# Taking 1/std out of the first MLP layer's input, and making the MLP matmuls narrower, in a one-core decode kernel

## The chip, the core and the metric

The kernel runs on one core of a Trainium2 chip. The metric is the device time of one execution in microseconds (us). Each execution is also reported with a "span", the time from the first to the last instruction of the program. Repeated executions of one kernel agree within some tenths of a microsecond out of 671 (the four of the kernel before within 0.18 us), so the noise is about 0.05%.

PE is the tensor engine, DVE the vector engine, ACT the scalar engine, POOL is GpSimd, SP the engine that issues most DMAs. SBUF is the memory that the kernel's transfers fill and its engines work from. Instructions wait for semaphores, which other instructions and transfers raise (in the trace a chunk of W2 does so in 16 steps). The granted clock is the share of its full speed that the tensor engine's clock was given, as the trace records it.

## The reference

A transformer block for 8 sequences, one new token each: a modulation from `c`, attention over a cache of 8192 keys and values, then an MLP. What matters here is the end:

```
x = x + ga * attention(...)                       # called x1 below
h = layernorm(x) * (1 + cb) + sb                  # layernorm: (x - mean) / sqrt(var + 1e-5)
hid = relu(h @ w1 + b1) ** 2                      # 512 -> 1792
x = x + gb * (hid @ w2 + b2)                      # 1792 -> 512
```

The two caches are 268 MB in bf16. `w1` and `w2` are 1.84 MB each.

## The kernel before

Keys and values stream through a ring of four SBUF slots, 4 MB per transfer, all issued by SP in one queue. The order of that queue at the end is: the last 4 MB of V in four pieces, then W1 in two, then W2 in four.

```python
d_w1 = [dma("sync", s_w1[i], ... W1v[:, a:z], w1_r[:, a:z] ...)
        for i, (a, z) in enumerate(((0, 3), (3, 4)))]
d_w2 = [dma("sync", s_w2[i], ...)          # rows f of W2, 128 each
        for i, (a, z, j) in enumerate(((0, 4, 4), (4, 8, 4), (8, 12, 4), (12, 14, 2)))]
```

After the last attention matmul and the output projection comes the tail. Activations are kept transposed (features on partitions, the batch of 8 in columns), and each weight tile of 128x128 is the stationary operand of one matmul. `wide` repeats the 8 columns four times, so that a matmul has 32 columns, of which 8 are used.

```python
t = vector(xcT = x1T - mean);  k_xc = t
t = vector(sqT = xcT * xcT)
t = vector(sqs = sum of sqT over k)
t = tensor(var_ps = ONESM.T @ sqs)                 # sum over partitions
k_xcb = vector(xcb = xcT * cb1)                    # cb1 = 1 + cb
t = scalar(std2 = sqrt(var_ps + eps))
t = vector(rstd2 = 1 / std2)
t = vector(h1T = xcb * rstd2)
k_hb = vector(hbT = h1T + mod(3))                  # mod(3) = sb
for ks in (range(KT - 1), range(KT - 1, KT)):      # KT = 4, FT = 14
    for f in range(FT):
        for k in ks:                               # waits for k_hb and W1's piece
            t = tensor(hT_w[f] += W1[k, f].T @ wide(hbT[k]))
        if k == KT - 1 and f % 7 == 6:             # one half of f is complete
            t = vector(rT = max(hT, 0));  k_sq.append(vector(hidT = rT * rT))
for f in range(FT):
    for k in range(KT):                            # waits for k_sq[f // 7] and d_w2[f // 4]
        t = tensor(yT_w[k] += W2[f, k].T @ wide(hidT[f]))
k_y2 = vector(y2T = yT * mod(5))                   # then two small transposes, copy, DMA out
```

(Shortened: every line is one instruction with its dependencies. The listing at the end of this section has the full text.)

Of the kernel before, what the change touches and what calls it, by code (L numbers as in the profile page):

```python
# [5 lines left out]
ACT = mybir.ActivationFunctionType  # L6
ALU = mybir.AluOpType
AX = mybir.AxisListType
FP32 = mybir.dt.float32
BF16 = mybir.dt.bfloat16  # L10
# [20 lines left out]
class Prog:  # L31
# [19 lines left out]
    def op(self, eng, fn, deps=(), chan=None):  # L51
        chan = chan or eng
        assert self.of[chan] == eng
        t = Tok(self.sems[chan], chan, self.at)
        t.used = chan in ("vecP", "scaP")
        self.ops[eng].append(Op(fn, deps, t, None, self.at))
        return t
# [95 lines left out]
def bass_adaLN_cond__gqa_block_cached__dense_activation_squared_relu__decode_kernel(  # L153
    nc, A_x, A_k_cache, A_v_cache, A_wq, A_wo, B_x, B_w1, B_b1, B_w2, B_b2, c, w_mod, out):
    B, _, D = A_x.shape
    _, HKV, SK, DH = A_k_cache.shape
# [4 lines left out]
    KT = D // 128  # L161
# [9 lines left out]
    with ExitStack() as es:  # L171
        E = es.enter_context
        sb = lambda name, shape, dt: E(nc.sbuf_tensor(name, shape, dt))
# [18 lines left out]
        IDENT = sb("IDENT", [128, 128], BF16)  # L192
# [6 lines left out]
        ONESM = sb("ONESM", [128, 128], FP32)  # L199
        ONESMB = sb("ONESMB", [128, 128], BF16)  # L200
        ONE8 = sb("ONE8", [1, B], BF16)
        PERM = sb("PERM", [128, 4, 32], BF16)
        oP = sb("oP", [128, 4, 6, B], BF16)
        epst = sb("epst", [128, 1], FP32)
# [8 lines left out]
        cb1 = sb("cb1", [128, KT, B], FP32)  # L213
        tmpT = sb("tmpT", [128, KT, B], FP32)
        haT = sb("haT", [128, KT, B], BF16)
        b1_row = sb("b1_row", [1, F], BF16)
# [3 lines left out]
        xcT = sb("xcT", [128, KT, B], FP32)  # L220
        sqT = sb("sqT", [128, KT, B], FP32)
        sqs = sb("sqs", [128, B], FP32)
        xcb = sb("xcb", [128, KT, B], FP32)
        std2 = sb("std2", [128, B], FP32)
        rstd2 = sb("rstd2", [128, B], FP32)
        h1T = sb("h1T", [128, KT, B], FP32)
        hbT = sb("hbT", [128, KT, B], BF16)
        hidT = sb("hidT", [128, FT, B], BF16)
        out_sb = sb("out_sb", [128, 256], BF16)

# [7 lines left out]
        rT = KF[:, 1024:1024 + 2 * FT * B].bitcast(FP32).rearrange("p (f b) -> p f b", f=FT)  # L238
# [7 lines left out]
        bank = lambda i: PS[:, i, :]  # L246
# [4 lines left out]
        op, dma = Pg.op, Pg.dma  # L251
# [34 lines left out]
        t = pool(lambda e: e.memset(ONE8[:], 1.0))  # L286
# [6 lines left out]
        t = select(IDENT[:], [[-1, 128]], 0, 1, 1.0, NE, t)  # L293
        t = select(IDF8[:], [[-1, 8]], 0, 1, 1.0, NE, t)
        k_id = t
        k_q0 = pool(lambda e: e.memset(QTm[:], 0.0))
        t = pool(lambda e: e.memset(Pm[:], 0.0), [t])
        k_pm = t
        for d in (-96, -64, -32, 0, 32, 64, 96):
            t = select(R4[:], [[-1, 128]], -d, 1, 1.0, NE, t)  # L300
        t = select(Qmask[:], [[-32, 4]], 0, 1, 0.0, GE, t)
        t = select(Qmask[:], [[32, 4]], 31, -1, 0.0, GE, t)
        for d in (0, 32, 64, 96):
            t = select(R4m[:], [[-1, 32]], -d, 1, 1.0, NE, t)

        for i in range(4):
            for cg in range(4):
                for half in range(2):
                    t = select(SEL[:, i, 4 * half:4 * half + 4], [[-1, 4]], -(32 * cg + 8 * i + 4 * half), 1,
                               1.0, NE, t)  # L310

        t = select(PERM[:], [[-1, 4], [-4, 32]], 0, 1, 1.0, NE, t)
# [31 lines left out]
        for k in range(KT):  # L344
            t = op("tensor", lambda e, k=k: e.matmul(csT_ps[:, k, :], cs_k[:, k, :], IDENT[0:B, 0:B],
                                                    is_transpose=True), [k_cs, k_id])
# [3 lines left out]
        for k in range(KT):  # L350
            t = op("tensor", lambda e, k=k: e.matmul(xT_ps[:, k, :], x_sb[:, k * 128:(k + 1) * 128],
                                                    IDENT[0:B, 0:B], is_transpose=True), [d_x])
        k_xT = op("vector", lambda e: e.tensor_copy(xT[:], xT_ps), [t])
        t = op("vector", lambda e: e.bn_stats(stats[:], x_sb), [d_x])
        t = op("vector", lambda e: e.bn_aggr(mv[:], stats[:]), [t])
        t = op("vector", lambda e: e.tensor_scalar(std_[:], mv[:, 1:2], EPS, None, ALU.add), [t])
        t = op("scalar", lambda e: e.activation(std_[:], std_[:], ACT.Sqrt), [t])
        t = op("vector", lambda e: e.reciprocal(rstd[:], std_[:]), [t])
        t = op("vector", lambda e: e.tensor_scalar(hn, x_sb, mv[:, 0:1], rstd[:, 0:1], ALU.subtract, ALU.mult), [t])
# [14 lines left out]
        for j in range(24):  # L374
            for k in range(KT):
                t = op("tensor", lambda e, j=j, k=k: e.matmul(
                    modT_ps[:, j, :], wm_cols(k, j), csT[:, k, :],
                    start=(k == 0), stop=(k == KT - 1)), [k_csT, d_wm])
        released[2] = t
        k_modT = op("vector", lambda e: e.tensor_copy(modT[:], modT_ps), [t])  # L380
        mod = lambda j: modT[:, KT * j:KT * (j + 1), :]
        t = op("vector", lambda e: e.tensor_scalar(ca1[:], mod(1), 1.0, None, ALU.add), [k_modT])
        t = op("vector", lambda e: e.tensor_tensor(tmpT[:], hnT_ps, ca1[:], ALU.mult), [t, k_hnT])
# [8 lines left out]
        for g in range(HKV):  # L392
            r0 = 16 * (g % 2) + 4 * (g // 2)
            k_QTm = op("vector", lambda e, g=g, r0=r0: e.tensor_copy(
                QTm[:, :, g, r0:r0 + REP], QT_ps[:, REP * g:REP * (g + 1), :].rearrange("p h b -> p b h")),
                [t, k_q0])
        k_cb1 = op("vector", lambda e: e.tensor_scalar(cb1[:], mod(4), 1.0, None, ALU.add))

        stg_free = [None, None, None, k_QTm]
# [14 lines left out]
        kt_read = [None, None]  # L414
        qn = 0
        norm_last = None

        def pe_fill(n, at=7):
            for _ in range(n):
                op("tensor", lambda e: e.matmul(bank(at)[:, 0:128], IDENT[:, :], IDENT[:, :]))  # L420

        def pe_stream(n, at):
            rhs = IDENT[:, :].unsqueeze(1).to_broadcast([128, 4, 128])
# [32 lines left out]
        def fcol(ap, f):  # L456
            a, j = (4 * (f // 4), 4) if f < F2 else (F2, 2)
            return ap[:, 128 * a:128 * (a + j)].rearrange("o (p j) -> o j p", j=j)[:, f - a, :]
# [1 line left out]
        wide = lambda ap: ap.unsqueeze(1).to_broadcast([128, 4, B])  # L460
        attn_w = bank(4)[:, 0:32 * KT].rearrange("p (k a b) -> p k a b", k=KT, a=4)
        attn_ps = attn_w[:, :, 0, :]
        hT_w = [bank(i)[:, 0:32 * 7].rearrange("p (f a b) -> p f a b", f=7, a=4) for i in range(2)]
        hT_ps = [h[:, :, 0, :] for h in hT_w]
        yT_w = bank(2)[:, 0:32 * KT].rearrange("p (k a b) -> p k a b", k=KT, a=4)
        yT_ps = yT_w[:, :, 0, :]

        def early(q0, q1, deps):
            nq = q1 - q0
# [18 lines left out]
        for b in range(B):  # L488
# [4 lines left out]
            for p in range(NP):  # L493
                n = 2 * NP * b + p
# [65 lines left out]
            for p in range(NP):  # L560
# [4 lines left out]
                if not lastu:  # L565
# [21 lines left out]
                    if lastb and p == 1:  # L587
                        k_oP = early(0, 2, [norm_last, k_all] + stg_free + hold)
                        for f in range(FT):
                            op("tensor", lambda e, f=f: e.matmul(  # L590
                                hT_ps[f // 7][:, f % 7, :], fcol(b1_row[:], f), ONE8[:, :],
                                start=(f % 7 == 0), stop=False, skip_group_check=True), [d_b2, s_bank_free[f // 7]])
                        project(0, 2, k_oP)
                    if lastb and p == 2:
# [67 lines left out]
        bc = lambda ap: ap.unsqueeze(1).to_broadcast([128, KT, B])  # L662
        t = op("vector", lambda e: e.tensor_tensor(xcT[:], x1T[:], bc(mean_ps), ALU.subtract), [t])
        k_xc = t
        t = op("vector", lambda e: e.tensor_tensor(sqT[:], xcT[:], xcT[:], ALU.mult), [t])
        t = op("vector", lambda e: e.tensor_reduce(sqs[:], sqT[:].rearrange("p k b -> p b k"), AX.X, ALU.add), [t])
        var_ps = bank(5)[:, 0:B]
        t = op("tensor", lambda e: e.matmul(var_ps, ONESM[:, :], sqs[:]), [t])  # L668
        k_xcb = op("vector", lambda e: e.tensor_tensor(xcb[:], xcT[:], cb1[:], ALU.mult), [k_xc])
        t = op("scalar", lambda e: e.activation(std2[:], var_ps, ACT.Sqrt, bias=epst[:, 0:1]), [t])  # L670
        t = op("vector", lambda e: e.reciprocal(rstd2[:], std2[:]), [t])
        t = op("vector", lambda e: e.tensor_tensor(h1T[:], xcb[:], bc(rstd2[:]), ALU.mult), [t, k_xcb])
        k_hb = op("vector", lambda e: e.tensor_tensor(hbT[:], h1T[:], mod(3), ALU.add), [t])
        k_sq = []
        wcol = lambda k, f: fcol(W1v[:, k, :], f)
        for ks in (range(KT - 1), range(KT - 1, KT)):
            for f in range(FT):
                for k in ks:
                    t = op("tensor", lambda e, f=f, k=k: e.matmul(  # L679
                        hT_w[f // 7][:, f % 7, :, :], wcol(k, f), wide(hbT[:, k, :]), start=False, stop=(k == KT - 1),  # L680
                        skip_group_check=True), [k_hb, d_w1[k // (KT - 1)]])
                if k == KT - 1 and f % 7 == 6:
                    hh = f // 7
                    fs = slice(7 * hh, 7 * (hh + 1))
                    t = op("vector", lambda e, hh=hh, fs=fs: e.tensor_scalar(
                        rT[:, fs, :], hT_ps[hh], 0.0, None, ALU.max), [t])
                    k_sq.append(op("vector", lambda e, fs=fs: e.tensor_tensor(
                        hidT[:, fs, :], rT[:, fs, :], rT[:, fs, :], ALU.mult), [t]))
        for f in range(FT):
            for k in range(KT):  # L690
                t = op("tensor", lambda e, f=f, k=k: e.matmul(  # L691
                    yT_w[:, k, :, :], W2v[:, f, k * 128:(k + 1) * 128], wide(hidT[:, f, :]),
                    start=False, stop=(f == FT - 1), skip_group_check=True), [k_sq[f // 7], d_w2[f // 4]])
        k_y2 = op("vector", lambda e: e.tensor_tensor(y2T, yT_ps, mod(5), ALU.mult), [t])
        outf = out.rearrange("b s d -> (b s) d")
# [45 lines left out]
```

## Time and profile before

| | before |
|---|---|
| time, median of 4 runs | 671.10 us (670.93 to 671.11) |
| span of the profiled run | 668.9 us |
| mean DMA rate | 424 GB/s |
| tail, from the start of x - mean to the start of the final multiply by gb | 659.3 to 666.0 us |

From the page of the kernel before: the busy share of the DMA engines and what they moved, in 40 equal slices of the span.

```profile
DMA  9999999999999999999999999999999999999996
GB/s 371 434 401 432 429 427 435 435 425 429 437 435 425 435 427 435 435 427 429 433 439 425 434 431 434 433 425 431 437 435 425 426 439 437 423 433 431 437 409 259
```

The DMA engines are at work through all of the run, at 424 GB/s on average, and they fall off in the last slice alone (16.7 us long). The kernel is bound by moving its 284 MB.

The timeline of the kernel before, in the tail. Columns: start in us, duration in us, engine, line, operation, output<-input, shapes, count, and in brackets how long the engine had been idle and what ended that.

```profile
660.04 0.60 PE L668 MATMUL PS<-sqs,ONESM 128*128 128x8 f32 x2 [0.53 <-DVE sqs L666]
660.67 0.27 ACT L670 ACTIVATE std<-PS,epst 128x8 f32<-128x8 f32 x1 [23.79 <-PE PS L668]
660.97 0.20 DVE L671 RECIPROCAL rstd<-std 128x8 f32<-128x8 f32 x1 [0.89 <-ACT std L670]
661.43 0.19 DVE L673 TENSOR_TENSOR hbT<-h1T,modT 128x32 bf16<-128x32 f32 x1
661.68 2.00 PE L679 MATMUL PS<-hbT,ring 128*128 128x32 bf16 x56 [1.05 <-DVE hbT L673]
664.01 1.91 PE L691 MATMUL PS<-hidT,ring 128*128 128x32 bf16 x56 [0.34 <-DVE hidT L687]
665.96 0.19 DVE L694 TENSOR_TENSOR KTb<-PS,modT 128x32 bf16<-128x32 f32 x1 [1.62 <-PE PS L691]
```

Read alone, this says that engines set the pace: layer 1 (L679) waits for hbT, which waits for 1/std; layer 2 (L691) waits for hidT. It is a nearly complete serial chain, and it looks as if whatever is cut out of it comes off the end. The chain of waits of the same kernel has one odd place, where layer 2 is in two pieces:

```profile
664.01 1.50 PE PS L691 x48
665.51 0.01 issue
665.52 0.41 PE PS L691 x8
```

48 matmuls and then 8. The first 48 use chunks 1 to 3 of W2 (f = 0 to 11), the last 8 use chunk 4. The starts of the matmuls in the trace show 26.7 ns between most, and 195 ns between the 48th and the 49th. (There is a slight wait for chunk 3 as well: 41 and 46 ns before the 33rd and the 34th.) The trace's DMA completion events say why. Each of these transfers has 16 of them, as many as the profile counts DMA engines, and they come apart: those of chunk 4 from 661.63 to 665.47 us, 3.8 us in all. The landing is the last of the 16:

```
last landing, us      V's last piece   W1 k=0..2   W1 k=3   W2 chunk 1   chunk 2   chunk 3   chunk 4
before                656.67           660.05      661.17   662.43       663.65    664.86    665.47
```

The 49th matmul starts at 665.52, 0.05 us behind chunk 4's landing.

### The profile page before, as it was taken

The page shows a single profiled execution, that of the slowest core. Times are in us where ns is not written, and L with a number is a line of the kernel's source. Part 1 is how long each engine was busy: PE and PEld are TensorE (multiplying, and loading weights), DVE is VectorE, ACT ScalarE, POOL GpSimd, SP SyncE. Part 2 cuts the span into 40 slices and gives each one's busy share as a digit, 9 for nine tenths or more (in the row PEclk, how much of TensorE's full clock was granted, in tenths as well). Part 3 has the DMA queues.
Part 4 walks back from the last instruction along what each step waited for, and adds up shares of the span by engine and source line. Part 5 has one row for each costly group of instructions (what it writes and reads, how often), then busy time and mean ns, then how long its engine had stood idle before and what let it go on. Part 6 is the DMA issues. An engine that isn't in the chain of part 4 may idle for free.

```text
span 668.9 us, 16187 instructions
## 1 busy us (share of the span) xinstructions
PE 495.5 (74%) x7492; PEld 341.1 (51%) x7492; DVE 298.4 (45%) x566; ACT 235.0 (35%) x280; POOL 16.7 (2%) x66
## 2 busy tenths in 40 slices
PE   2394964799639983699647996399846996489976
PEld 2383731676318751477316762287414772167634
DVE  2162741466316661267414672166613673156722
ACT  2061630365106640166204660056402662046600
POOL 7200000000000000000000000000000000000000
PEclk9996995699869997699967997599966999689986
DMA  9999999999999999999999999999999999999996
GB/s 371 434 401 432 429 427 435 435 425 429 437 435 425 435 427 435 435 427 429 433 439 425 434 431 434 433 425 431 437 435 425 426 439 437 423 433 431 437 409 259
DMA packets 12969, 283.95 MB, mean 424 GB/s; under 512 B 1266, under 2 KB 2323, under 8 KB 4372
## 3 DMA queue, kind: packets, MB, share of 16 engines
q1 hardware_dynamic: 12900, 283.65, 99.1%
q8 instruction: 13, 0.21, 0.1%
q14 instruction: 8, 0.07, 0.0%
q10 hardware_dynamic: 48, 0.02, 0.0%
HBM read 283.66 MB, written 0.01 MB: 424 GB/s over the span
## 4 chain that ended last, share of the span: by engine, by line
PE 50%; DMA 41%; DVE 5%; ACT 2%; issue 1%; SPq 0%
DMA ring<-in_A_k_cache_dram 37%; PE PS L434 35%; PE PS L449 9%; DMA ring<-in_A_v_cache_dram 4%; DVE Pm L540 3%; PE PS L568 3%; ACT KTb L439 1%; ACT P_sb L518 1%; DVE m L454 1%; PE PS L527 1%; PE PS L425 0%; PE PS L547 0%; PE PS L626 0%; PE PS L691 0%; PE PS L679 0%
## 5 line engine op out<-in xcount | busy, mean ns | idle before, releaser
L439 ACT ACTIVATE KTb<-PS 128x1024 bf16<-128x1024 bf16 x192 | 196.7, 1024 | 375.7 <-PE PS L434 375.7
L434 PE MATMUL PS<-IDENT,ring 128*128 128x128 bf16 x4096 | 267.0, 227 | 51.6 <-DMA ring<-in_A_k_cache_dram 51.6
L434 PEld LDWEIGHTS PS<-IDENT,ring 128*128 128x128 bf16 x4096 | 246.3, 102 | 100.3 <-DMA ring<-in_A_k_cache_dram 53.6
L441 DVE COPY KTb<-PS 128x1024 bf16<-128x1024 bf16 x320 | 210.0, 687 | 151.5 <-PE PS L434 149.3
L568 PE MATMUL PS<-ring,Pm 128*32 128x512 bf16 x992 | 83.1, 494 | 63.6 <-DMA ring<-in_A_v_cache_dram 62.7
L577 DVE CAST O_sb<-PS 128x512 bf16<-128x512 f32 x31 | 21.4, 692 | 144.9 <-PE PS L568 144.9
L449 PE MATMUL PS<-KTb,Qb 128*32 128x512 bf16 x1024 | 79.1, 386 | 4.5 <-ACT KTb L439 4.5
L568 PEld LDWEIGHTS PS<-ring,Pm 128*32 128x32 bf16 x992 | 29.5, 117 | 102.5 <-DMA ring<-in_A_v_cache_dram 64.1
L425 PE MATMUL PS<-IDENT 128*128 128x512 bf16 x120 | 31.3, 380 | 0.0
L581 PEld LDWEIGHTS PS<-SEL,O_sb 128*128 128x128 bf16 x124 | 5.3, 99 | 45.0 <-DVE O_sb L577 45.0
L518 ACT ACTIVATE P_sb<-PS,negm 128x512 bf16<-128x512 f32 x32 | 21.6, 686 | 18.9 <-DVE negm L514 18.9
L581 PE MATMUL PS<-SEL,O_sb 128*128 128x8 bf16 x124 | 8.0, 170 | 24.8 <-DVE O_sb L577 24.8
L449 PEld LDWEIGHTS PS<-KTb,Qb 128*32 128x32 bf16 x1024 | 15.4, 94 | 21.1 <-ACT KTb L439 8.5
L540 DVE COPY Pm<-PS 64x512 bf16<-64x512 bf16 x48 | 19.5, 419 | 13.4 <-PE PS L527 12.4
L454 DVE TENSOR_REDUCE m<-PS 128x1 f32<-128x512 f32 x32 | 22.0, 689 | 6.6 <-PE PS L449 6.6
L527 PE MATMUL PS<-IDENT,P_sb 128*64 128x128 bf16 x512 | 20.4, 222 | 2.0 <-ACT P_sb L518 1.2
L527 PEld LDWEIGHTS PS<-IDENT,P_sb 128*64 128x64 bf16 x512 | 15.2, 109 | 9.8 <-ACT P_sb L518 9.8
L425 PEld LDWEIGHTS PS<-IDENT 128*128 128x128 bf16 x120 | 9.9, 103 | 10.8 <-issue 3.4
L584 DVE TENSOR_TENSOR oTn<-PS,rinv 128x8 bf16<-128x8 f32 x31 | 6.0, 193 | 10.9 <-PE PS L581 10.9
L537 ACT ACTIVATE Pm<-PS 64x512 bf16<-64x512 bf16 x16 | 9.5, 593 | 1.1
L388 PE MATMUL PS<-haT,ring 128*128 128x8 bf16 x128 | 3.6, 168 | 7.7 <-DMA ring<-in_A_wq_dram 7.7
L670 ACT ACTIVATE std<-PS,epst 128x8 f32<-128x8 f32 x1 | 0.3, 268 | 23.8 <-PE PS L668 23.8
(112 smaller groups left out, 97.9 us busy)
## 6 DMA issues: line engine op xcount, KB each, us to landing
ring<-in_A_k_cache_dram SPq DMA_DIRECT2D x32, 4096.0 KB, 34.9
ring<-in_A_v_cache_dram SPq DMA_DIRECT2D x31, 4096.0 KB, 28.3
ring<-in_A_wq_dram SPq DMA_DIRECT2D x1, 4096.0 KB, 20.7
ring<-in_w_mod_dram SPq DMA_DIRECT2D x1, 3072.0 KB, 10.6
wo_sb<-in_A_wo_dram SPq DMA_DIRECT2D x1, 3072.0 KB, 45.4
ring<-in_A_v_cache_dram SPq DMA_DIRECT2D x1, 2048.0 KB, 23.7
ring<-in_B_w_dram SPq DMA_DIRECT2D x3, 512.0 KB, 17.6
ring<-in_B_w_dram SPq DMA_DIRECT2D x1, 1344.0 KB, 21.2
```

What stands on the lines that cost most here:

```text
L425: op("tensor", lambda e: e.matmul(bank(at).rearrange("p (a r) -> p a r", a=4), IDENT[:, :], rhs))
L434: t = op("tensor", lambda e, j=j, i=i: e.matmul(STG[j][:, i, :], src[:, 32 * k + 8 * j + i, :], IDENT[:, :], is_transpose=True), [loaded[n ...
L439: stg_free[j] = op("scalar", lambda e, j=j, dst=dst: e.activation(dst, STG[j], ACT.Copy), [t], "scaP")
L441: stg_free[j] = op("vector", lambda e, j=j, dst=dst: e.tensor_copy(dst, STG[j]), [t], "vecP")
L449: t = op("tensor", lambda e, hf=hf, q=q, rhs=rhs: e.matmul(PS[32 * q:32 * (q + 1), k, :], Qb[:, 2 * p + hf, :], rhs, start=(p == 0 and hf ...
L454: return op("vector", lambda e: e.tensor_reduce(m4[:, k:k + 1], bank(k), AX.X, ALU.max), [t])
L518: exps.append(op("scalar", lambda e, k=k: e.activation(P_sb[:, k, :], bank(k), ACT.Exp, bias=negm[:, 0:1], scale=inv_sqrt, accum_out=rs4[: ...
L527: t = op("tensor", lambda e, k=k, i=i, hf=hf, src=src: e.matmul(STG[k][64 * hf:64 * (hf + 1), i, :], src, IDENT[:, :], is_transpose=True, ...
L540: done.append(op("vector", lambda e, dst=dst, frm=frm: e.tensor_copy(dst, frm), [t, k_pm], "vecP"))
L568: t = op("tensor", lambda e, p=p, m=m, cg=cg, vt=vt, Obank=Obank: e.matmul(Obank[32 * cg:32 * (cg + 1), :], lhs[:, p, 32 * m:32 * m + 32], ...
L577: t = op("vector", lambda e, osb=osb, Obank=Obank: e.tensor_copy(osb, Obank), [t], "vecP")
L581: t = op("tensor", lambda e, i=i, osb=osb, oT_ps=oT_ps: e.matmul(oT_ps, osb[:, i * 128:(i + 1) * 128], SEL[:, i, :], start=(i == 0), stop= ...
```

## The change

The first MLP layer is linear in its input, and 1/std is one number per sequence, hence per column. So (xc * (1 + cb) / std + sb) @ W1 + b1 equals (xc * (1 + cb)) @ W1 / std + (sb @ W1 + b1). The change puts xc * (1 + cb) and sb side by side as 16 columns under the same weights, starts layer 1 before the variance is known, and multiplies by 1/std afterwards. The intent is to take the variance's chain out of the way of layer 1, and to stop paying for columns that aren't used.

```diff
+        k_sb = op("vector", ... tensor_copy(hbT[:, :, 1, :], mod(3)))      # at start-up
...
+        k_hb = op("vector", ... tensor_tensor(hbT[:, :, 0, :], xcT[:], cb1[:], ALU.mult), [t])
         t = op("vector", ... sqT = xcT * xcT)
-        t = op("vector", ... sqs = sum of sqT)
-        t = op("tensor", ... var_ps);  xcb;  std2;  rstd2;  h1T = xcb * rstd2;  hbT = h1T + mod(3)
+        k_sqs = op("vector", ... sqs = sum of sqT)
-        for ks in (range(KT - 1), range(KT - 1, KT)):
+        for k in range(KT):
+            if k == KT - 1:
+                t = op("tensor", ... var_ps, ONESM, sqs, [k_sqs])
+                t = op("scalar", ... std2 = sqrt(var_ps + eps))
+                k_rstd = op("vector", ... rstd2 = 1 / std2)
             for f in range(FT):
-                for k in ks: matmul(hT_w[f], wcol(k, f), wide(hbT[:, k, :]))       # 32 columns
+                matmul(hT_ps[f], wcol(k, f), hbT[:, k, :, :])                     # 16 columns
                 if k == KT - 1 and f % 7 == 6:
-                    rT = max(hT, 0);  hidT = rT * rT
+                    rT = hT[.., 0, ..] * rstd2;  rT = rT + hT[.., 1, ..];  hidT = max(rT, 0) * rT
         for f in range(FT):
-            matmul(yT_w[k], W2[f, k], wide(hidT[:, f, :]))                         # 32 columns
+            matmul(yT_ps[k], W2[f, k], hidT[:, f, :])                              # 8 columns
```

(The bias of layer 1 now goes into the second half of the 16 columns, and a helper that nobody called is deleted.)

More of the change, by code (lines that the diff above doesn't have):

```diff
@@ L222, in bass_adaLN_cond__gqa_block_cached__dense_activation_squared_relu__decode_kernel @@
         sqs = sb("sqs", [128, B], FP32)
-        xcb = sb("xcb", [128, KT, B], FP32)
         std2 = sb("std2", [128, B], FP32)
         rstd2 = sb("rstd2", [128, B], FP32)
-        h1T = sb("h1T", [128, KT, B], FP32)
-        hbT = sb("hbT", [128, KT, B], BF16)
+        hbT = sb("hbT", [128, KT, 2, B], BF16)
         hidT = sb("hidT", [128, FT, B], BF16)
@@ L396, in bass_adaLN_cond__gqa_block_cached__dense_activation_squared_relu__decode_kernel @@
                 [t, k_q0])
+        k_sb = op("vector", lambda e: e.tensor_copy(hbT[:, :, 1, :], mod(3)))
         k_cb1 = op("vector", lambda e: e.tensor_scalar(cb1[:], mod(4), 1.0, None, ALU.add))
@@ L416, in bass_adaLN_cond__gqa_block_cached__dense_activation_squared_relu__decode_kernel @@
         norm_last = None
-        def pe_fill(n, at=7):
-            for _ in range(n):
-                op("tensor", lambda e: e.matmul(bank(at)[:, 0:128], IDENT[:, :], IDENT[:, :]))
         def pe_stream(n, at):
@@ L462, in bass_adaLN_cond__gqa_block_cached__dense_activation_squared_relu__decode_kernel @@
         attn_ps = attn_w[:, :, 0, :]
-        hT_w = [bank(i)[:, 0:32 * 7].rearrange("p (f a b) -> p f a b", f=7, a=4) for i in range(2)]
-        hT_ps = [h[:, :, 0, :] for h in hT_w]
-        yT_w = bank(2)[:, 0:32 * KT].rearrange("p (k a b) -> p k a b", k=KT, a=4)
-        yT_ps = yT_w[:, :, 0, :]
+        hT_ps = [bank(i)[:, 0:16 * 7].rearrange("p (f a b) -> p f a b", f=7, a=2) for i in range(2)]
+        yT_ps = bank(2)[:, 0:KT * B].rearrange("p (k b) -> p k b", k=KT)
         def early(q0, q1, deps):
@@ L590, in bass_adaLN_cond__gqa_block_cached__dense_activation_squared_relu__decode_kernel @@
                             op("tensor", lambda e, f=f: e.matmul(
-                                hT_ps[f // 7][:, f % 7, :], fcol(b1_row[:], f), ONE8[:, :],
+                                hT_ps[f // 7][:, f % 7, 1, :], fcol(b1_row[:], f), ONE8[:, :],
                                 start=(f % 7 == 0), stop=False, skip_group_check=True), [d_b2, s_bank_free[f // 7]])
@@ L664, in bass_adaLN_cond__gqa_block_cached__dense_activation_squared_relu__decode_kernel @@
         k_xc = t
-        t = op("vector", lambda e: e.tensor_tensor(sqT[:], xcT[:], xcT[:], ALU.mult), [t])
-        t = op("vector", lambda e: e.tensor_reduce(sqs[:], sqT[:].rearrange("p k b -> p b k"), AX.X, ALU.add), [t])
+        k_hb = op("vector", lambda e: e.tensor_tensor(hbT[:, :, 0, :], xcT[:], cb1[:], ALU.mult), [t])
+        t = op("vector", lambda e: e.tensor_tensor(sqT[:], xcT[:], xcT[:], ALU.mult), [k_xc])
+        k_sqs = op("vector", lambda e: e.tensor_reduce(sqs[:], sqT[:].rearrange("p k b -> p b k"), AX.X, ALU.add), [t])
         var_ps = bank(5)[:, 0:B]
-        t = op("tensor", lambda e: e.matmul(var_ps, ONESM[:, :], sqs[:]), [t])
-        k_xcb = op("vector", lambda e: e.tensor_tensor(xcb[:], xcT[:], cb1[:], ALU.mult), [k_xc])
-        t = op("scalar", lambda e: e.activation(std2[:], var_ps, ACT.Sqrt, bias=epst[:, 0:1]), [t])
-        t = op("vector", lambda e: e.reciprocal(rstd2[:], std2[:]), [t])
-        t = op("vector", lambda e: e.tensor_tensor(h1T[:], xcb[:], bc(rstd2[:]), ALU.mult), [t, k_xcb])
-        k_hb = op("vector", lambda e: e.tensor_tensor(hbT[:], h1T[:], mod(3), ALU.add), [t])
         k_sq = []
         wcol = lambda k, f: fcol(W1v[:, k, :], f)
-        for ks in (range(KT - 1), range(KT - 1, KT)):
+        rsb = rstd2[:].unsqueeze(1).to_broadcast([128, 7, B])
+        for k in range(KT):
+            if k == KT - 1:
+                t = op("tensor", lambda e: e.matmul(var_ps, ONESM[:, :], sqs[:]), [k_sqs])
+                t = op("scalar", lambda e: e.activation(std2[:], var_ps, ACT.Sqrt, bias=epst[:, 0:1]), [t])
+                k_rstd = op("vector", lambda e: e.reciprocal(rstd2[:], std2[:]), [t])
             for f in range(FT):
-                for k in ks:
-                    t = op("tensor", lambda e, f=f, k=k: e.matmul(
-                        hT_w[f // 7][:, f % 7, :, :], wcol(k, f), wide(hbT[:, k, :]), start=False, stop=(k == KT - 1),
-                        skip_group_check=True), [k_hb, d_w1[k // (KT - 1)]])
+                t = op("tensor", lambda e, f=f, k=k: e.matmul(
+                    hT_ps[f // 7][:, f % 7, :, :], wcol(k, f), hbT[:, k, :, :], start=False, stop=(k == KT - 1),
+                    skip_group_check=True), [k_hb, k_sb, d_w1[k // (KT - 1)]])
                 if k == KT - 1 and f % 7 == 6:
@@ L684, in bass_adaLN_cond__gqa_block_cached__dense_activation_squared_relu__decode_kernel @@
                     fs = slice(7 * hh, 7 * (hh + 1))
-                    t = op("vector", lambda e, hh=hh, fs=fs: e.tensor_scalar(
-                        rT[:, fs, :], hT_ps[hh], 0.0, None, ALU.max), [t])
-                    k_sq.append(op("vector", lambda e, fs=fs: e.tensor_tensor(
-                        hidT[:, fs, :], rT[:, fs, :], rT[:, fs, :], ALU.mult), [t]))
+                    t = op("vector", lambda e, hh=hh, fs=fs: e.tensor_tensor(
+                        rT[:, fs, :], hT_ps[hh][:, :, 0, :], rsb, ALU.mult), [t, k_rstd])
+                    t = op("vector", lambda e, hh=hh, fs=fs: e.tensor_tensor(
+                        rT[:, fs, :], rT[:, fs, :], hT_ps[hh][:, :, 1, :], ALU.add), [t])
+                    k_sq.append(op("vector", lambda e, fs=fs: e.scalar_tensor_tensor(
+                        hidT[:, fs, :], rT[:, fs, :], 0.0, rT[:, fs, :], ALU.max, ALU.mult), [t]))
         for f in range(FT):
@@ L691, in bass_adaLN_cond__gqa_block_cached__dense_activation_squared_relu__decode_kernel @@
                 t = op("tensor", lambda e, f=f, k=k: e.matmul(
-                    yT_w[:, k, :, :], W2v[:, f, k * 128:(k + 1) * 128], wide(hidT[:, f, :]),
+                    yT_ps[:, k, :], W2v[:, f, k * 128:(k + 1) * 128], hidT[:, f, :],
                     start=False, stop=(f == FT - 1), skip_group_check=True), [k_sq[f // 7], d_w2[f // 4]])
```

## The prediction

> **What bounds the kernel now.** The span is 668.9 us (671.09 us measured). The page's DMA row is at 9 tenths in nearly every slice, 424 GB/s on average: almost the whole run streams the K and V caches, which the change leaves alone. It touches the tail, about 659.3 to 666.2 us in the timeline: variance, hbT, layer 1 (56 matmuls), ReLU and square, layer 2 (56 matmuls).
>
> There the chain of waits is drawn through engines: xcT done 659.53, square, sum, ones-matmul (0.61), sqrt (0.28), reciprocal (0.21), two vector steps (0.20 each), layer 1 from 661.68 to 663.47, two vector steps of 0.23, layer 2 from 664.01. But weights are still arriving. The DMA completion events give the last landings: W1 rows k=0..2 at 660.05, k=3 at 661.17; W2's four chunks at 662.43, 663.65, 664.86 and 665.47. Layer 2 already stalls for the last chunk: its 49th matmul comes 0.195 us after the 48th, at 665.52, just behind 665.47. So W2's landing ends last, not the engines.
>
> **What the change removes, adds, moves.**
> 1. Layer 1 need not wait for the variance. hbT is ready at about 659.75 (one 0.19 us multiply after xcT); W1's landing makes the start 660.1, 1.6 us earlier.
> 2. The ones-matmul now stands behind 42 of 56 matmuls: 660.1 plus 42 at 33 ns is 661.5. Then 0.61 + 0.28 + 0.21 and gaps: 1/std at about 662.65, after the last layer-1 matmul.
> 3. Three vector instructions per half instead of two, about 0.23 each: layer 2 can start at about 663.4 instead of 664.01. Of 1.6 us, 0.6 survive to there.
> 4. Narrow matmuls: no gain in rate. At full clock the 32-wide and the 8-wide output-projection matmuls both start every 25 ns; at granted clock 0.5, 32-wide layer 2 takes 26.7 ns, as the 8-wide modulation matmuls do at start-up. Layer 1 takes 33 ns because its weights are read with a stride (its last two column groups, of smaller stride, take 27). [...] Only the last matmul's latency shrinks: 188 to about 168 ns, 0.02 us.
> 5. One more vector copy (0.17 us) at start-up, in idle time: nothing.
>
> **On the critical path.** Layer 2's groups f=8..11 wait for 664.86 and f=12..13 for 665.47. The last 8 matmuls start at 665.52 as before. The 0.6 us becomes waiting inside layer 2 (0.2 us becomes 0.6 to 0.8). Gain at the end 0.02 to 0.05 us, below the spread of runs (0.18 us).
>
> **Predicted time** 671.0 us, range 670.4 to 671.7. Chances: faster by over 2% 0.01, within 2% 0.98, slower by over 2% 0.01.
>
> **What would show each step.** Layer 1 starting near 660.1, right behind W1's landing; ones-matmul near 661.5; 1/std near 662.65; layer 2 near 663.4; spacing still 33 and 26.7 ns (granted clock 0.5); gaps in layer 2 before the 33rd and 49th matmul, ended by DMA; the last matmul and final vector multiply within 0.1 us of before, relative to the end of the V stream.
>
> **What would make it wrong.** If the clock returns to full near 663.4[...]: about 0.1 us more. If W2 lands earlier in other executions, so that the engines end last: up to 0.6 us (0.1%). If the cache stream shifts: several us either way, for which I see no reason.

The sum is before's 671.09 us less a gain of 0.02 to 0.05 us, so 671.0. The 663.4 us for a return of the clock is an estimate from the trace of before: its last change there is at 660.00 us, the two before it are at 653.17 and 656.59, and 3.41 us more is 663.4. The 0.1 us is 56 matmuls at 26.7 less 25 ns.

## The result, and the profile after

| | before | after |
|---|---|---|
| time, median of 4 runs | 671.10 us (670.93 to 671.11) | 670.66 us (670.64 to 670.72) |
| span of the profiled run | 668.9 us | 668.8 us |
| layer 1 starts | 661.68 | 660.00 |
| layer 2 starts | 664.01 | 663.35 |
| W2's chunk 4 has landed | 665.47 | 665.38 |
| final multiply by gb starts | 665.96 | 665.84 |

The ratio is 0.9994, with a 95% interval of 0.9977 to 1.0012. It is the mean time of one kernel's fast runs over that of the other's of the same rounds, so not quite the ratio of the medians above. Executions over 1.5% slower than the fastest of the same kernel are left out of the means.

The timeline of the kernel after, the lines that answer to those of before (hbT is L658, layer 1 L671, the ones-matmul L667, layer 2 L685, the final multiply L688):

```profile
659.42 0.19 DVE L658 TENSOR_TENSOR hbT<-xcT,cb 128x32 bf16<-128x32 f32 x1
660.00 1.50 PE L671 MATMUL PS<-hbT,ring 128*128 128x16 bf16 x42 [0.64 <-DVE sqs L660]
661.36 0.57 PE L667 MATMUL PS<-sqs,ONESM 128*128 128x8 f32 x2
661.78 0.59 PE L671 MATMUL PS<-hbT,ring 128*128 128x16 bf16 x14
662.27 0.20 DVE L669 RECIPROCAL rstd<-std 128x8 f32<-128x8 f32 x1 [2.32 <-ACT std L668]
662.58 0.22 DVE L677 TENSOR_TENSOR KTb<-PS,rstd 128x56 f32<-128x56 f32 x1
662.83 0.21 DVE L679 TENSOR_TENSOR KTb<-KTb,PS 128x56 f32<-128x56 f32 x1
663.08 0.22 DVE L681 SCALAR_TENSOR_TENSOR hidT<-KTb 128x56 bf16<-128x56 f32 x1
663.35 1.02 PE L685 MATMUL PS<-hidT,ring 128*128 128x8 bf16 x32 [0.98 <-DVE hidT L681]
664.79 1.01 PE L685 MATMUL PS<-hidT,ring 128*128 128x8 bf16 x24 [0.42 <-DMA ring<-in_B_w_dram]
665.84 0.19 DVE L688 TENSOR_TENSOR KTb<-PS,modT 128x32 bf16<-128x32 f32 x1 [1.92 <-PE PS L685]
```

Layer 1 starts 1.7 us earlier by the clock of the trace, and layer 2 0.66 us earlier. But layer 2 is now in pieces, 32 matmuls and then 24, and the second piece waits for a DMA from W2. Within those 24 the trace's starts show a second gap, before the 49th matmul. The two gaps are 0.591 and 0.214 us, against one of 0.195 before. The bracket at L671 names sqs, but layer 1 does not wait for sqs: by the edit it waits for hbT (done at 659.61), the copy of sb and W1. In the seven profiles of after and its variants in which layer 1 runs before the ones-matmul, it starts 0.135 or 0.136 us behind the landing of W1's first piece (659.87 in after), so W1 is what holds it. The page now draws the chain that ended last through the weights:

```profile
651.18 14.19 DMA ring<-in_B_w_dram
665.38 0.05 issue
665.42 0.39 PE PS L685 x8
665.81 0.02 issue
665.84 0.20 DVE KTb L688
```

The last 8 matmuls of layer 2 start 0.046 us behind the landing of chunk 4 in both kernels, by the trace's own starts in ns.

Because the V stream does not land at the same moment in every execution, the tables below count from the landing of V's last piece (656.67 us before, 656.53 after). Counted so, layer 1 starts 5.01 us after it before and 3.47 after, so 1.54 us sooner; layer 2 at 7.34 and 6.82, so 0.52 sooner; the final multiply at 9.29 and 9.31, not sooner at all. (Differences of such rounded figures can be off by 0.01.)

### The profile page after: what moved, and what is told of

It reads as the page before. It is cut to its first block, busy times and chain, and to the rows that moved or that the text cites. A ratio compares the mean times of both kernels' runs of the same rounds, so it can differ in the third digit from the quotient of the medians.

```text
span 668.8 us, 16189 instructions
## 1 busy us (share of the span) xinstructions
PE 495.9 (74%) x7492; PEld 341.4 (51%) x7492; DVE 298.8 (45%) x567; ACT 235.1 (35%) x280; POOL 16.9 (3%) x66
## 4 chain that ended last, share of the span: by engine, by line
PE 50%; DMA 39%; DVE 5%; ACT 2%; SPq 2%; issue 1%
DMA ring<-in_A_k_cache_dram 37%; PE PS L429 36%; PE PS L444 9%; DVE Pm L533 3%; PE PS L561 2%; DMA ring<-in_B_w_dram 2%; SPq L602 2%; ACT KTb L434 1%; ACT P_sb L511 1%; DVE m L449 1%; PE PS L520 1%; PE PS L420 1%; PE PS L540 0%; DVE rhs_r L537 0%; DVE Dm L502 0%
```

## The experiments

Every kernel was run five times beside the kernel before on the same chip, with one profiled execution each. The theory is that the landing of W2's last chunk sets the end, and that the change turned its gain into waiting inside layer 2. The rivals are that the engines still bind and the change pays its gain back with its own extra work, and that the width of the matmuls is what counts. "Few" in a label means that chunks 3 and 4 of W2 are not loaded, so that the weights end early and the engines' chain alone sets the end. Their outputs are wrong, which doesn't matter for the times.

Times in us. The first four columns are from the trace, counted from the landing of V's last piece; the time and span are means of the runs, with the mean time of before in the same rounds last.

| run | layer 1 | layer 2 | last W2 landing | final multiply | time | span | before |
|---|---|---|---|---|---|---|---|
| before (profiled run) | 5.01 | 7.34 | 8.80 | 9.29 | | | |
| after (profiled run) | 3.47 | 6.82 | 8.85 | 9.31 | | | |
| after_again | 3.47 | 6.82 | 8.81 | 9.27 | 670.73 | 668.86 | 671.06 |
| before_few | 5.02 | 7.36 | 6.83 | 9.05 | 670.73 | 668.60 | 671.06 |
| after_few | 3.46 | 6.81 | 6.84 | 8.50 | 670.01 | 668.10 | 671.06 |
| after_delay | 3.49 | 7.24 | 9.14 | 9.60 | 670.90 | 669.14 | 671.06 |
| after_slow_recip | 3.51 | 7.40 | 8.83 | 9.29 | 670.77 | 668.92 | 670.89 |
| before_slow_recip | 5.55 | 7.88 | 8.79 | 9.60 | 671.48 | 669.36 | 670.89 |
| before_plus3 | 5.01 | 7.35 | 8.80 | 9.28 | 670.55 | 668.80 | 670.89 |
| before_narrow_few | 5.01 | 7.33 | 6.86 | 9.02 | 670.74 | 668.64 | 670.89 |
| after_varfirst_few | 3.85 | 6.39 | 6.88 | 8.19 | 669.81 | 667.92 | 671.11 |
| after_lanes8 | 3.43 | 6.78 | 11.56 | 12.02 | 673.57 | 671.70 | 671.11 |
| before_lanes8 | 5.03 | 7.36 | 11.57 | 12.04 | 673.94 | 671.84 | 671.11 |
| after_pool_copy | 3.49 | 6.83 | 8.84 | 9.31 | 670.47 | 668.74 | 670.91 |

### 1. The changed kernel again

No edit.

> The changed kernel again, unedited, to see whether the 0.44 us of the first comparison repeats. Theory (W2's last landing sets the end): the trace's final vector multiply stays within 0.1 us of the kernel before, relative to the landing of the last V chunk, and the time is 0 to 0.5 us shorter, all of it from when the stream itself lands. Rival (the shorter engine chain is what shows): the final multiply comes 0.4 us or more earlier relative to that landing.

The final multiply is at 9.27, against 9.29 before: the tail is not shorter. The time is 0.33 us under before's all the same (ratio 0.9996, interval 0.9982 to 1.0009). Every run has its own span, so the difference can be split: the spans differ by 0.08 us (668.86 against 668.94), and the time outside the span by 0.24 us (1.87 against 2.11). So the theory holds for the tail, and a part of the gain that it did not foresee lies outside the span. The interval includes 1, so the times alone do not settle a difference this small; but the time outside the span repeats, at 2.09 to 2.12 us for before in all four rounds of experiments and at 1.85 and 1.87 us for after in its two comparisons. Experiments 7 and 12 look at that.

In this execution the granted PE clock was at half from 650.85 us on, while in the first profiled runs it was back at full between 656.59 and 660.00. The end came at the same place, so the clock in that stretch does not set it either.

### 2 and 3. Weights that end early

```diff
-  enumerate(((0, 4, 4), (4, 8, 4), (8, 12, 4), (12, 14, 2)))]
+  enumerate(((0, 4, 4), (4, 8, 4)))]
-  W2v[:, f, ...]   ... d_w2[f // 4]
+  W2v[:, f % 8, ...]   ... d_w2[f % 8 // 4]
```

> Before, without the last two chunks of W2 (f=8..13 read the rows of f=0..5, so the result is wrong on purpose). Theory: the engines' chain of before was only 0.2 us behind the weights, so it is exposed: 0.15 to 0.25 us shorter than before from V's landing to the final multiply, and layer 2 runs without a gap at 26.7 ns from about 664.0. Rival (engines bind in before): no change, 0.0 us.

> After, without the same two chunks (wrong on purpose). Theory: the engines' chain of after is 0.75 us ahead of the weights: 0.7 to 0.8 us shorter than after from V's landing to the final multiply, and 0.6 to 0.7 us shorter than before_few. Rival (the change's own costs eat its gain): at most 0.2 us shorter than before_few.

The timeline of layer 2 in before_few, and then in after_few:

```profile
663.88 1.66 PE L691 MATMUL PS<-hidT,ring 128*128 128x32 bf16 x56 [0.34 <-DVE hidT L687]
```

```profile
663.42 1.66 PE L685 MATMUL PS<-hidT,ring 128*128 128x8 bf16 x56 [0.97 <-DVE hidT L681]
```

In both, layer 2 runs its 56 matmuls in one piece in 1.66 us: the gaps are gone with the weights that caused them. Before gains 0.24 us by it and after 0.81 us. With the weights out of the way after is ahead by 0.55 us from V's landing to the final multiply, and by 0.50 us of span. That is a little less than the 0.6 to 0.7 expected, because the expectation took the 0.66 us that layer 2 started earlier by the trace's clock, of which 0.14 was an earlier V stream. The change's own gain is real, and the weights hide it.

What each kernel gains is what its layer 2 had waited. From its first to its last start layer 2 takes 1.717 us in before and 1.483 in before_few, 2.282 us in after and 1.490 in after_few: 0.23 and 0.79 us of waiting.

### 4. A delay behind the reciprocal

```diff
+  t = op("vector", lambda e: e.tensor_copy(std2[:], rstd2[:]), [t])
+  k_rstd = op("vector", lambda e: e.tensor_copy(rstd2[:], std2[:]), [t])
```

> After, with two more dependent vector copies (about 0.46 us) behind the reciprocal; the result stays right. Theory: layer 2 starts 0.46 us later, its wait before the 33rd matmul shrinks from 0.59 to about 0.13 us, and the end does not move: 0.00 to 0.05 us. Rival (engines bind): 0.46 us longer.

This missed. Layer 2 started 0.42 us later, but the end also moved, by 0.28 us of span in the mean and by 0.29 us from V's landing (9.60). Taken alone it speaks for the rival. But the trace shows another cause: the wait before the 33rd matmul shrank to 0.171 us as the theory has it, and the 49th still started 0.05 us behind the landing of chunk 4. It was the landing that was late, at 9.14 us after V in place of 8.85. The chain of waits of this run:

```profile
651.23 14.48 DMA ring<-in_B_w_dram
665.71 0.05 issue
665.76 0.39 PE PS L687 x8
```

The DMA view of the window 664.5 to 665.5 us of after_delay (columns: queue and kind, packets, MB, share) shows what came between; in the same window of after there is no q14 line:

```profile
q1 hardware_dynamic: 7, 0.01, 2.7%
q14 instruction: 1, 0.01, 2.0%
```

The q14 packet is a fetch of 8 KB of instructions that started at 664.96 us and took 0.328 us. In after, the corresponding fetch starts at 669.88 us, after the last instruction. With it, chunk 4's last completion came 0.93 us behind chunk 3's, in place of 0.64, while the other fifteen, in order, came 0.62 to 0.67 us behind (0.61 to 0.69 in after). The last packet of W2 had started on time, 8.39 us after V's landing (8.38 in after), and the fetch started 0.006 us behind it; only the completion was late. The fetch's 0.33 us is near the 0.29 us lost. That the fetch sat on the engine with the last of W2 is inferred from this; the trace does not name the engine.

### 5 and 6. The same delay without a new instruction

To test that, the reciprocal is made slower: it is taken over 96 columns, of which 8 matter (the other 88 are ones).

```diff
-  std2 = sb("std2", [128, B], FP32)          rstd2 = sb("rstd2", [128, B], FP32)
+  std2 = ONES[:, 0:B]                        rstd2 = sb("rstd2", [128, 96], FP32)
-  e.reciprocal(rstd2[:], std2[:])
+  e.reciprocal(rstd2[:], ONES[:, 0:96])
```

> After, with the reciprocal of 1/std made over 96 columns in place of 8 (result right, no instruction added), so that it takes 0.4 to 0.6 us longer. The first delay, by two added vector copies, moved the end by 0.3 us; its trace shows an 8 KB instruction fetch at 664.96 us, in the last weights, that the others have after the end. Theory: that fetch, not the delay, moved the last landing; here no fetch falls before 668 us, layer 2 starts 0.4 to 0.6 us later, the wait before its 33rd matmul shrinks from 0.59 to under 0.2 us, and the span stays within 0.1 us of after (668.85). Rival (the engines bind after all): span 0.3 to 0.6 us longer.

> Before, with the same slower reciprocal (right, no instruction added). Theory: before has only 0.2 us of waiting in layer 2 to hide it, so the span grows by the delay less 0.2 us: 0.2 to 0.4 us longer than before's 668.95, and the gap before the 49th matmul of layer 2 is gone. Rival (weights bind before just as far as after): under 0.1 us.

The reciprocal took 0.75 us in place of 0.20 in both. The chain of waits of after_slow_recip, and then of before_slow_recip:

```profile
662.46 0.76 DVE rstd L669
664.08 1.44 PE PS L685 x48
...
665.56 0.39 PE PS L685 x8
...
665.97 0.20 DVE KTb L688
```

```profile
661.40 0.77 DVE rstd L671
664.99 1.69 PE PS L691 x56
...
666.71 0.20 DVE KTb L694
```

In after, layer 2 starts 0.58 us later, the gap before the 33rd matmul is gone, the one before the 49th is 0.200 us, and the final multiply is at 9.29: all 0.58 us are absorbed. The span is 668.92, against 668.86 in experiment 1. (Against before in the same rounds it is 0.12 us longer, and in experiment 1 it was 0.08 us shorter. The two profiled spans differ by 0.13 us, and 0.12 of it lies before V's landing, so it is not the tail that grew.) No 8 KB fetch fell into the tail (the next is at 670.00); a 16 KB fetch of another queue starts in the tail of every run (at 662.65 here, 662.47 in after), so it does not make the difference. So the delay costs nothing, and what experiment 4 paid for was not the delay.

In before, layer 2 starts 0.54 us later, runs in one piece, and the end moves by 0.31 us: 0.23 us are absorbed, which is what layer 2 had waited in before (1.717 less 1.483 us). The span grew by more, 0.56 us in the mean against the same rounds where 0.2 to 0.4 was expected, with single runs from 668.9 to 669.7. In the profiled run V itself landed 0.44 us later than in the first profile of before, so part of that is the stream. The tail's 0.31 is the figure to trust.

### 7. Three more vector instructions where they cost nothing

```diff
+  for spare in (xcb, h1T, xcT):
+      op("vector", lambda e, spare=spare: e.tensor_copy(spare[:], mod(3)))     # at start-up
```

> Before, with three vector copies to scratch at start-up, in idle time (right; the same number of vector instructions as in the delayed kernel). Theory of the fetch: the 8 KB instruction fetch moves from 670.5 us, after the end, to about 664 to 665 us; the span grows by up to 0.33 us although nothing in the tail changed, and the time outside the span shrinks from about 2.1 to about 1.75 us, so that the time hardly moves. Rival (instruction count is nothing): span and time within 0.1 us of before.

Half of it missed. The fetch moved, but to 668.01 us, behind the last work of the engines (666.84) and shortly before the output's last landing (668.23), and not into the tail; and the tail is that of before (9.28). But the time outside the span did fall, from 2.09 to 1.75 us, and with it the time by 0.34 us, to 670.55. So the kernel before, with three useless copies, measures as much faster as the changed kernel does. The 0.3 to 0.4 us by which after is ahead need not have anything to do with the MLP.

### 8. The width alone

```diff
-  hT_w[f // 7][:, f % 7, :, :], wcol(k, f), wide(hbT[:, k, :])
+  hT_ps[f // 7][:, f % 7, :], wcol(k, f), hbT[:, k, :]
-  yT_w[:, k, :, :], W2v[:, f, ...], wide(hidT[:, f, :])
+  yT_ps[:, k, :], W2v[:, f % 8, ...], hidT[:, f, :]           # and two chunks of W2 left out
```

> Before without the last two chunks of W2 (wrong on purpose), so that the engines' chain sets the end, and with all MLP matmuls 8 wide in place of 32. Theory: spacing stays 33 ns in layer 1 and 26.7 ns in layer 2; from the variance's end to the final vector multiply it is only 0.04 us shorter than with 32 wide (two latencies of 0.02). Rival (the width is what the change gains by): 0.4 us shorter or more, spacing 25 ns or less.

Layer 1 in before_few, 32 wide (its layer 2 is shown in experiment 2), and then layers 1 and 2 in before_narrow_few, 8 wide:

```profile
661.54 1.99 PE L679 MATMUL PS<-hbT,ring 128*128 128x32 bf16 x56 [1.05 <-DVE hbT L673]
```

```profile
661.52 1.98 PE L677 MATMUL PS<-hbT,ring 128*128 128x8 bf16 x56 [1.05 <-DVE hbT L671]
663.84 1.65 PE L689 MATMUL PS<-hidT,ring 128*128 128x8 bf16 x56 [0.34 <-DVE hidT L685]
```

A quarter of the columns, and 0.01 us less per 56 matmuls. The spacing is 33 and 26.7 ns in both, and the final multiply is 0.03 us earlier (9.02 against 9.05), where 0.04 was expected. In before's trace each of the 56 matmuls of a layer has its own 128x128 weight load (about 118 ns long in layer 1 and 104 in layer 2, overlapping); the width, at least, is not what sets the spacing here.

### 9. Where the other microsecond went

```diff
-            if k == KT - 1:
+            if k == 0:                      # the ones-matmul, sqrt and reciprocal of the variance
```

> After without the last two chunks of W2 (wrong on purpose, so that the engines' chain sets the end), with the ones-matmul of the variance put before layer 1 in place of behind its 42nd matmul. The sum for it is ready at about 660.0, just when W1 lands. Theory: its place behind the 42 matmuls is what ate 1 us of the 1.6 us that layer 1 starts earlier; in front, 1/std is ready before layer 1 ends, layer 2 starts 0.3 to 0.4 us earlier, counted from the landing of the last V chunk, and the end moves as much against after_few. Rival (its place is nothing, since it must run anyway): under 0.1 us.

The timeline of after_varfirst_few:

```profile
660.23 0.50 PE L667 MATMUL PS<-sqs,ONESM 128*128 128x8 f32 x2 [0.64 <-DVE sqs L660]
660.58 1.96 PE L671 MATMUL PS<-hbT,ring 128*128 128x16 bf16 x56
661.07 0.20 DVE L669 RECIPROCAL rstd<-std 128x8 f32<-128x8 f32 x1 [0.90 <-ACT std L668]
663.12 1.76 PE L685 MATMUL PS<-hidT,ring 128*128 128x8 bf16 x56 [0.59 <-DVE hidT L681]
```

1/std is ready 1.1 us before it is used (661.27 against 662.35), layer 2 starts 0.42 us sooner than in after_few, and the end comes 0.31 us sooner. There a gap of 0.113 us opens before the 17th matmul of layer 2, where chunk 2 of W2 begins: the weights bind again as soon as the engines get ahead. Layer 1 came 1.54 us sooner and layer 2 only 0.52, so 1.02 us was lost between them; the place of the ones-matmul accounts for 0.42 of it. The rest is not taken apart by a run of its own, but the table gives it. In after_varfirst_few the ones-matmul stands in front, and layer 1 starts 0.39 us later than in after_few (3.85 against 3.46). From layer 1's start to layer 2's it takes 2.54 us against 2.34 in before_few: about 0.2 us, near the 0.25 us from start to start of the third vector instruction per half. The three together, 0.39, 0.42 and 0.2, make up the loss.

### 10 and 11. The weights' end moved on purpose

The completions of chunk 4 are far apart: in after the first of the 16 comes at 661.64 us, the tenth at 663.02 and the last at 665.38. If the late ones could be avoided, the end might come sooner. The edit loads the chunk 8 partitions at a time. What the author assumed of the engines that such small transfers take is not shown by any run, and it is cut from the first expectation; "those 8 engines" there are the assumed ones. What the trace of after_lanes8 shows is a count: each of the 16 small transfers gave one early step of its semaphore at issue and 8 later ones, where the one transfer of after gave 16 completions.

```diff
-  ... (8, 12, 4), (12, 14, 2)))]
+  ... (8, 12, 4)))]
+  for q in range(0, 128, 8):
+      d_last = dma("sync", s_w2[3], lambda e, q=q: e.dma_start(W2v[q:q + 8, 12:14, :] ..., B_w2[...][q:q + 8]))
+  d_w2.append(d_last)
```

> After, with the last W2 chunk (256 KB, f=12..13) loaded by 16 transfers of 8 partitions each[...], in place of one over all 16 (result right, same bytes). Ten of the 16 completions of that chunk come by 663.1 us and six between 663.7 and 665.4. Theory (the slowest lanes' last landing is the end): if those 8 engines are among the early ten, the last landing becomes that of the third chunk, 664.75, and the end comes 0.5 to 0.6 us earlier; if they are not, the landing and the end both move later, by 0.5 us or more. Rival (engines bind): no change either way.

> Before with the same splitting of the last W2 chunk (right, same bytes). If the landing comes 0.6 us earlier, the engines' chain of before, only 0.2 us behind the weights, gains 0.2 us and no more, so that after_lanes8 is 0.3 to 0.4 us of span shorter than this. If the landing comes later, both end alike, within 0.1 us of each other from V's landing on. Rival (engines bind in both): after_lanes8 and this differ as after and before do, under 0.1 us, and neither moves.

Layer 2 of after_lanes8 in the timeline, and then of before_lanes8:

```profile
663.60 1.19 PE L690 MATMUL PS<-hidT,ring 128*128 128x8 bf16 x32 [0.96 <-DVE hidT L686]
665.57 0.59 PE L690 MATMUL PS<-hidT,ring 128*128 128x8 bf16 x16 [0.78 <-DMA ring<-in_B_w_dram]
668.42 0.37 PE L690 MATMUL PS<-hidT,ring 128*128 128x8 bf16 x8 [2.27 <-DMA ring<-in_B_w_dram]
```

```profile
664.24 1.04 PE L696 MATMUL PS<-hidT,ring 128*128 128x32 bf16 x32 [0.34 <-DVE hidT L692]
665.63 0.61 PE L696 MATMUL PS<-hidT,ring 128*128 128x32 bf16 x16 [0.36 <-DMA ring<-in_B_w_dram]
668.49 0.39 PE L696 MATMUL PS<-hidT,ring 128*128 128x32 bf16 x8 [2.25 <-DMA ring<-in_B_w_dram]
```

As a way to a faster kernel it failed: the landing came at 11.56 us after V in place of 8.85. Which engines were used, and whether they are among the early ones, is not shown, and the splitting has costs of its own: in after_lanes8 the last data packet of W2 ends 1.21 us later than in after (9.59 against 8.39 us after V), and the landing follows it by 1.96 us in place of 0.46, with the last completions coming 0.177 us apart. As a test of what follows the landing it is plain. The landing moved by 2.7 us and the end moved with it, by 2.7 us in both kernels, and the two end alike (12.02 and 12.04) though their layers 2 start 0.58 us apart. It does not show what set the end before the landing was moved: a landing this late would set the end even where the engines had set it. That rests on experiments 2, 3, 5 and 6.

### 12. The same vector instructions as before

```diff
-  k_sb = op("vector", lambda e: e.tensor_copy(hbT[:, :, 1, :], mod(3)))
+  k_sb = op("gpsimd", lambda e: e.tensor_copy(hbT[:, :, 1, :], mod(3)), [k_modT])
```

> After, with the start-up copy of the shift into hbT made by GpSimd in place of the vector engine (right), so that the vector engine runs exactly as many instructions as before. Theory: the 0.3 to 0.4 us by which after measures shorter lie 0.24 us outside the span and come from the one more vector instruction, which moves the program's last 8 KB instruction fetch from 1.6 us to 1.1 us after the span's end. Then here the fetch is back at 1.6 us, the time outside the span back at 2.05 to 2.2 us (after: 1.82 to 1.90), the span stays at 668.7 to 669.0, and the time is within 0.15 us of before. Rival (the gain is the change's own work): outside 1.85 us as in after, and the time 0.3 to 0.4 us under before.

This missed on every count but the span. The fetch stayed at 669.89 us, 1.13 us behind the span's end, and the time outside the span fell further, to 1.73 us. The assumption about the count was wrong too: the trace has 573 vector records in before, 575 in after and 574 here. The time is 670.47 us, 0.44 us under before, with a tail as long as before's (9.31).

## Why the prediction was right, and where it was off

**What sets the end.** The prediction said that the landing of W2 ends last. It was right: the end came sooner only when the weights ended early (2, 3), did not follow a delay of 0.58 us of the engines in after (5), and followed one of 0.54 us in before only by what went past its 0.23 us of waiting (6). Where the landing moved, by 0.3 us (4) and by 2.7 us (10, 11), the end stayed 0.46 to 0.48 us behind it.

**The engines' chain.** Layer 1 was foreseen at 660.1 and came at 660.00; the ones-matmul at 661.5 (661.36); 1/std at 662.65 (662.47, its start plus its duration); layer 2 at 663.4 (663.35). That 0.6 of 1.6 us survive up to layer 2 was confirmed, as 0.52 of 1.54 us when both are counted from V's landing. That the times agree so closely by the clock of the trace is in part luck, since V landed 0.14 us earlier than in the profile that the prediction was made from: counted from V, layer 2 was foreseen at 6.73 and came at 6.82.

**Where the gain went.** The prediction had it become waiting in layer 2, 0.2 us turning into 0.6 to 0.8. The gaps less the usual 0.027 us are 0.17 us before and 0.56 + 0.19 = 0.75 us after, before the 33rd and the 49th matmul as foreseen; with the small ones they come to 0.23 and 0.79 us (2, 3). With fewer weights the gain came out at the end: 0.55 us (3).

**Narrow matmuls.** No gain in rate was foreseen and none came (8). In before's trace 8 and 32 columns both take 25 ns from start to start at full clock in the output projection (L644 and L483). At the half clock of the tail (0.5 from 660.00 us on) they take 26.7 ns alike in layer 2, where the weights of neighbouring columns lie side by side. Layer 1 (L679) takes 33 ns where its weights are read with a step of four bf16 elements between columns, and about 27 in its last two column groups, where the step is two.

**The size.** The prediction gave 0.02 to 0.05 us of gain and 671.0 us; it was 0.33 to 0.44 us and 670.66, within the range of 670.4 to 671.7. The term that was mis-sized is one that the sum did not have. It took the time outside the span as the same for both kernels, and this was 2.11 us for before and 1.87 us for after. Spans alone differ by 0.08 us, near what was foreseen and less than the spread of before's own spans (668.5 to 669.1 in those rounds). The 0.24 us need not be the work of the MLP: three idle copies bring before to 1.75 us (7), and moving one copy to another engine brings after to 1.73 us (12). What makes the time outside the span 1.73 or 2.11 us stays open. I argued for the last instruction fetch, and experiment 12 does not bear that out. The record does show a pattern: before and its four variants in which that fetch starts 1.62 or 1.63 us behind the end of the profiled span have means of 2.09 to 2.13 us outside the span, and all other kernels, where it starts earlier, have 1.73 to 1.91. What links the two is not shown.

## What to carry to other kernels

When a chain of engines runs next to a stream of weights, compare the landing of each piece with the start of the instruction that uses it before costing a cut in the chain: here a chain that looked serial already spent 0.2 us waiting for the weights, and a true gain of 0.5 us became waiting. Here a matmul with its own 128x128 weights cost the same with 8 columns as with 32 (26.7 or 33 ns from start to start), so narrowing it bought nothing. And a difference of a few tenths of a microsecond should be split into span and rest, and an added instruction's mere presence should be tried, before it is credited to a change.
